# A new order table for an attention, Fourier and feed-forward kernel: TensorE's narrow products stand in fewer, longer runs

## The chip, the core and the metric

The kernel runs on one NeuronCore of a Trainium2 chip. Five engines work side by side, each on its own queue of instructions in a fixed order: TensorE (PE: matrix products; PEld is its loading of weights), VectorE (DVE), ScalarE (ACT), GpSimd (POOL) and SyncE (SP, which here only issues DMAs). They wait for one another through semaphores. The metric is the device time of one execution in microseconds, lower is better.

## The reference

```python
# sliding-window attention, 8 batches, 8 heads, 576 positions, 64 columns
scores = (1.0 / np.sqrt(D)) * np.matmul(q, k.transpose(0, 1, 3, 2))
mask = (rel >= 0) & (rel < 64)
attn = softmax(np.where(mask, scores, -1e9))
x = np.matmul(attn, v)            # as (8, 576, 512)
# Fourier mixing, norm and feed-forward
X = np.fft.fft(np.fft.fft(x, axis=1), axis=2)
u = x + np.real(X)
un = (u - mean(u)) / np.sqrt(var(u) + 1e-6)
out = u + np.maximum(un @ w_ch1, 0.0) @ w_ch2      # 512 -> 2048 -> 512
```

Inputs arrive as float32 (the two weight matrices as float64 bits), the output is float32.

## The kernel before

The 4608 rows of the problem are 36 attention tiles of 128 positions. For each tile and each of two groups g of four heads, `score` (L648 in float32 for tiles 0 to 12, L653 in two float16 parts from tile 13 on) makes the scores psc, DVE adds the mask and takes the maximum (L670), ACT takes the exponential (L678), the result pr is turned around (through TensorE, L689 pp, in the early tiles; as two float16 parts that are made by ACT, DVE or POOL and turned by a DMA in the later ones) into pt, and `av` (L732) multiplies it by the values into pa. After that come `normed` (DVE, L738 to L742), the Fourier transform of each batch (pg L963, pz L997), the norm, and the feed-forward of 18 chunks of 256 rows: a first product ph (L1283; 12 products of 256 columns for one f), the two-part relu hh (ACT L1292, then DVE L1295), and a second product po (L1264; 6 products of 512 columns for one f). Chunk 0 runs it in float32, the others in three float16 passes. In this text the number behind a name is the tile, chunk or batch: psc22_1 is the score of tile 22, group 1.

Two kinds of attention product use only a part of TensorE's array: pa and the later psc work on 128 rows by 64 columns (two products beside each other, for the two halves of a tile), the early psc on 64 by 64. The page writes that as 128*64 and 64*64 behind the name. They are called narrow here, everything else (128*128, and the 97*96 of the Fourier stage) is called full.

What sets the order is written out: `op` records 2900 steps with their reads and writes, `follow` walks them in the order of the table ORDER, and the program is issued in just that order, on all engines. SECOND lists the steps with two possible engines that go to their second one (ACT or DVE, DVE or POOL). `follow` keeps a planned time too; where TensorE is planned to stand idle for more than 0.8 us before the float16 feed-forward begins, the last loop puts products into the gap that serve nothing but TensorE's clock (warm, L1359). Each psum tile comes from a ring of banks: ps (4 banks: scores, pa, turns, Fourier), f1 (2: ph) and f2 (2: po).

Of the kernel before, what the change touches and what calls it, by code (L numbers as in the profile page):

```python
# [58 lines left out]
171 10 0 8 172 1 7 9 4 3 173 174 175 196 176 177 197 180 181 179 178 199 185 182 198 200 201 186 183 222 202 184 187  # L59
11 205 188 191 210 221 189 206 211 226 204 190 203 207 192 247 193 208 224 223 209 212 227 12 13 213 214 16 225 14 230  # L60
2 215 15 246 251 235 216 228 231 236 194 248 17 232 237 217 229 18 21 195 233 218 249 234 250 238 239 272 252 240 255
253 19 241 271 256 20 260 257 26 276 22 277 258 23 219 5 242 220 259 243 261 273 264 274 265 254 262 275 31 27 263 280
24 244 6 281 266 245 282 487 267 268 25 283 278 36 284 285 269 270 28 490 286 488 298 491 299 287 489 289 288 312 290
291 279 303 292 41 492 302 493 293 306 496 512 307 294 497 513 295 316 300 296 304 494 317 308 515 46 498 301 305 313
517 310 538 499 309 322 314 500 37 318 537 505 501 323 319 518 324 51 315 325 502 506 542 47 326 503 514 311 543 540
327 504 32 331 563 33 29 335 56 332 34 320 333 336 321 562 541 337 507 297 516 328 334 508 495 521 329 61 38 42 567
330 52 339 39 338 340 57 519 43 341 509 66 522 343 539 526 523 44 342 35 53 344 71 527 345 30 520 54 524 664 565 48
510 566 49 568 528 76 355 350 529 525 346 546 511 665 347 40 530 351 547 667 58 348 668 352 548 81 62 63 349 549 64
353 550 59 354 532 531 45 369 72 50 77 86 78 370 82 73 564 74 372 371 83 544 84 373 91 533 67 68 375 79 87 69 555 534
551 377 96 556 552 669 689 376 75 88 374 356 553 101 570 554 55 380 60 545 97 690 80 92 98 382 670 93 99 106 535 102  # L70
378 89 357 575 362 381 571 379 65 94 111 70 557 358 694 576 558 692 666 103 95 577 559 385 100 104 359 116 386 695 107
108 572 360 569 383 112 714 109 363 384 121 85 390 117 578 118 536 361 560 113 573 717 119 574 114 105 579 364 126 387
110 580 718 122 123 561 671 673 693 365 715 124 366 581 90 392 367 582 131 115 678 583 391 674 679 127 584 128 393 585
129 120 136 586 125 680 388 130 588 394 132 589 719 389 133 675 395 134 141 590 681 587 396 592 691 591 137 596 400
593 594 138 135 146 598 401 142 139 672 740 143 140 676 597 602 144 677 151 603 720 682 147 145 684 148 698 739 149
595 683 150 397 697 599 368 413 600 414 398 604 415 152 716 153 154 742 402 605 699 156 685 700 416 611 417 686 423
403 612 155 601 613 608 399 424 161 157 405 609 158 606 696 610 425 607 767 687 703 617 688 426 721 743 159 621 404
427 162 166 163 744 160 406 164 618 766 428 165 619 614 429 745 407 430 620 615 768 167 439 168 2020 704 440 169 2016
441 616 622 442 701 170 2017 623 443 705 418 624 2018 444 625 769 2019 419 408 626 770 420 702 627 421 445 2021 772
422 446 723 431 411 706 2026 432 409 433 2027 2022 434 410 455 2023 771 2024 435 456 436 457 875 2032 437 458 628 2025  # L80
438 459 460 447 707 448 461 2030 2028 724 773 449 709 708 725 2031 741 2029 450 878 2033 722 879 728 451 910 726 462
2036 727 452 412 2034 2044 629 876 729 2035 710 2037 453 774 471 454 730 472 463 746 2038 464 473 2042 474 465 466 475
2039 775 476 467 468 477 748 2040 478 469 2043 2041 470 2045 630 479 2048 2046 731 2049 480 636 2047 481 732 2050 631
733 482 734 632 483 2054 735 765 881 484 2056 637 485 2051 633 634 749 2055 2052 2053 750 643 635 2057 753 486 2060
2058 638 754 2059 751 639 711 640 755 2061 756 641 644 642 2062 712 2063 650 759 2066 645 2068 2064 2067 646 2072 736
2069 651 2073 2070 752 2071 652 737 647 747 757 777 2084 2074 648 758 882 649 2076 760 2085 713 657 883 2075 2077 653
911 778 654 2078 761 2082 655 658 656 2079 2083 884 2080 659 2081 762 2086 776 877 2090 738 763 779 2088 660 2087 764
661 781 802 2089 885 782 916 787 662 2094 783 880 788 917 789 2096 784 918 790 2091 785 886 2097 786 2092 791 807 2093
889 792 2095 890 806 2065 891 2102 810 912 811 2098 2100 803 913 945 2099 892 914 895 793 896 795 893 915 2101 794 897
816 796 980 2108 898 797 888 2103 948 780 820 899 919 798 2104 2106 799 804 900 808 2109 949 2105 812 920 2107 805 946  # L90
809 2120 2110 800 950 814 813 930 921 2112 894 817 951 821 931 924 887 2113 818 663 925 822 826 823 2111 926 2121 815
827 983 828 952 829 2122 2123 2124 830 927 831 984 953 903 932 2114 819 1090 835 824 825 985 933 839 836 801 837 981
# [1298 lines left out]
```

## Time and profile before

| what | value |
|---|---|
| runs | 989.87, 994.36, 994.63 us; median 994.36 us |
| profiled execution | 990.8 us, of which the span of the trace is 988.6 us |
| PE busy | 964.2 us, 98% of the span |
| DVE, ACT, POOL busy | 644.1, 367.1, 332.3 us |
| granted TensorE clock, mean over the span | 0.996 |

The page counts an engine as busy from the start of its instructions to their ends. Matmuls are pipelined: the start of one matmul to the start of the next is the time that it costs, while the duration shown for it (0.2 to 0.4 us) overlaps with its neighbours'. So the working of this text goes by starts. [...]

### The profile page before, as it was taken

The page shows a single profiled execution, that of the slowest core. Times are in us where ns is not written, and L with a number is a line of the kernel's source. Part 1 is how long each engine was busy: PE and PEld are TensorE (multiplying, and loading weights), DVE is VectorE, ACT ScalarE, POOL GpSimd, SP SyncE. Part 2 cuts the span into 40 slices and gives each one's busy share as a digit, 9 for nine tenths or more (in the row PEclk, how much of TensorE's full clock was granted, in tenths as well). Part 3 has the DMA queues.
Part 4 walks back from the last instruction along what each step waited for, and adds up shares of the span by engine and source line. Part 5 has one row for each costly group of instructions (what it writes and reads, how often), then busy time and mean ns, then how long its engine had stood idle before and what let it go on. Part 6 is the DMA issues. An engine that isn't in the chain of part 4 may idle for free.

```text
span 988.6 us, 22785 instructions
## 1 busy us (share of the span) xinstructions
PE 964.2 (98%) x8964; PEld 672.2 (68%) x8964; DVE 644.1 (65%) x1827; ACT 367.1 (37%) x853; POOL 332.3 (34%) x675
## 2 busy tenths in 40 slices
PE   7699999999999999999999999999999999999998
PEld 6577667676766676666776667666776677666665
DVE  5699888988768668867658565776756555421111
ACT  5565657844433343334324443224422221111110
POOL 1342152233834541342643264425623331210000
PEclk9899999999999999999999999999999999999999
DMA  9998664526897958778669754876354401320010
GB/s 206 240 236 227 175 175 106 132 59 135 154 195 147 176 86 184 144 170 156 111 145 166 139 125 113 172 141 146 65 132 92 87 1 52 69 43 12 1 43 22
DMA packets 309067, 123.09 MB, mean 125 GB/s; under 512 B 291096, under 2 KB 291224, under 8 KB 308960
## 3 DMA queue, kind: packets, MB, share of 16 engines
q1 hardware_dynamic: 306240, 112.72, 53.9%
q0 software_dynamic: 2720, 8.92, 3.5%
q8 instruction: 70, 1.15, 0.5%
q14 instruction: 37, 0.30, 0.1%
HBM read 54.99 MB, written 14.17 MB: 70 GB/s over the span
## 4 chain that ended last, share of the span: by engine, by line
PE 85%; DMA 6%; DVE 5%; ACT 2%; issue 1%; POOL 1%; SPq 0%; DVEq 0%; POOLq 0%; ACTq 0%
PE ph L1283 36%; PE po L1264 35%; PE pa L732 3%; PE psc L653 2%; PE pz L997 2%; PE pg L963 2%; DMA kn<-in_k 2%; PE psc L648 1%; DMA mt<-md,gix 1%; DMA uhl<-up 1%; DMA qbd<-flex 1%; PE pp L689 1%; PE py L823 1%; PE mt L1040 1%; PE warm L1359 1%
## 5 line engine op out<-in xcount | busy, mean ns | idle before, releaser
L1264 PE MATMUL po<-w1s,hh 128*128 128x512 f16 (+1 forms) x1696 | 426.2, 388 | 1.5 <-ACT hh L1289 0.9
L1283 PE MATMUL ph<-uhl,w0s 128*128 128x256 f16 (+1 forms) x3384 | 424.1, 277 | 1.9 <-DVE hh L1295 1.1
L1283 PEld LDWEIGHTS <-w0s 128*128 128x128 f16 x3264 | 316.5, 98 | 81.2 <-issue 3.5
L1264 PEld LDWEIGHTS <-hh 128*128 128x128 f16 x1632 | 154.5, 98 | 139.6 <-DVE hh L1295 1.0
L1292 ACT ACTIVATE hh<-ph 128x512 f16<-128x512 f32 x136 | 80.9, 595 | 330.1 <-PE ph L1283 252.0
L1295 DVE SCALAR_TENSOR_TENSOR hh<-ph,hh 128x512 f16<-128x512 f32 x136 | 93.4, 687 | 156.7 <-ACT hh L1292 156.5
L678 ACT ACTIVATE pr<-pr,nm 128x128 f32<-128x128 f32 x288 | 91.2, 390 | 43.1 <-DVE nm L670 41.8
L670 DVE CUSTOM_DVE_ANT_0 pr<-psc,mskb 128x128 f32<-128x128 f32 x288 | 65.6, 286 | 23.6 <-PE psc L653 18.9
L1071 POOL DMA_INDIRECT mt<-md,gix x34 | 34.6, 1019 | 112.4 <-DMA md<-mp 49.0
L489 POOL TENSOR_TENSOR flex<-pr,flex 128x128 f16<-128x128 f32 x112 | 49.9, 476 | 54.8 <-ACT flex L479 44.9
L1095 POOL TENSOR_TENSOR rs<-mv,mhalf 128x1 f32<-128x1 f32 x36 | 23.4, 649 | 102.9 <-DVE mv L1091 88.5
L489 POOL TENSOR_TENSOR up<-un,up 128x128 f16<-128x128 f32 x80 | 36.4, 485 | 47.8 <-ACT up L479 36.4
L489 POOL TENSOR_TENSOR flex<-qn,flex 128x128 f16<-128x128 f32 x80 | 36.5, 491 | 28.6 <-ACT flex L479 24.8
L732 PE MATMUL pa<-ve,pt 128*64 128x65 f16 (+1 forms) x760 | 43.6, 207 | 1.9 <-ACT pt L479 0.9
L489 POOL TENSOR_TENSOR flex<-kn,flex 128x128 f16<-128x128 f32 x60 | 27.9, 494 | 48.8 <-ACT flex L479 30.4
L732 PE MATMUL pa<-va,pt 128*64 128x65 f16 (+1 forms) x760 | 43.7, 207 | 0.0
L479 ACT CAST up<-un 128x512 f16<-128x512 f32 x29 | 17.8, 615 | 48.3 <-DVE un L1099 19.3
L489 POOL TENSOR_TENSOR y<-xu 128x128 f32<-128x128 f32 x36 | 19.3, 568 | 44.8 <-DVE xu L742 39.6
L489 POOL TENSOR_TENSOR hs<-h,hs 128x97 f16<-128x97 f32 x56 | 21.4, 415 | 37.5 <-ACT hs L479 32.2
L742 DVE TENSOR_TENSOR xu<-pa,rc 128x256 f32<-128x256 f32 x72 | 30.6, 424 | 2.5
L1318 DVE SCALAR_TENSOR_TENSOR xu<-po,osc,xu 128x512 f32<-128x512 f32 x34 | 24.2, 744 | 11.1 <-PE po L1264 11.1
L653 PEld LDWEIGHTS <-qbd 128*64 128x64 f16 x736 | 21.9, 110 | 13.8 <-issue 13.7
(163 smaller groups left out, 1172.4 us busy)
## 6 DMA issues: line engine op xcount, KB each, us to landing
wd<-in_moe_w_ch SPq DMA_DIRECT2D x20, 512.0 KB, 5.4
out<-xu SPq DMA_DIRECT2D x36, 256.0 KB, 2.6
ve<-va SPq DMA_DIRECT2D x67, 130.0 KB, 3.4
kn<-in_k SPq DMA_DIRECT2D x32, 256.0 KB, 3.6
qn<-in_q SPq DMA_DIRECT2D x32, 256.0 KB, 4.0
flex<-in_moe_w_ch SPq DMA_DIRECT2D x12, 512.0 KB, 7.8
flex<-in_v SPq DMA_DIRECT2D x20, 256.0 KB, 3.3
md<-mp SPq DMA_DIRECT2D x24, 192.0 KB, 2.6
```

Of the source, the lines that this page charges most:

```text
L489: eng.tensor_tensor(out=out[:, k : k + w], in0=in0[:, k : k + w], in1=in1[:, k : k + w], op=al)
L653: nc.tensor.matmul(out, qbd[i][:, jj, h, 64 * z : 64 * z + 64], keys(h, jj), start=(z == 0), stop=(z == 1))
L670: nc.vector.tensor_tensor_reduce(out=t["pr", g][:, hp], in0=t["ps", g][:, hp], in1=mskb[:, m : m + P], scale=-0.125, scalar=3.0e38, op0=AL ...
L678: nc.scalar.activation(pr, pr, AF.Exp, bias=t["nm", g][:, hp : hp + 1], scale=-1.0)
L732: nc.tensor.matmul(pa[sl, hp], pt[:, sl], v_, start=(x == 0), stop=(x == len(mm) - 1))
L742: nc.vector.tensor_tensor(out=xv[:, g::2], in0=pa[:, :, 0:64], in1=rc.to_broadcast([P, 4, 64]), op=ALU.mult)
L1071: nc.gpsimd.indirect_dma_start(out=mts[T], out_offset=None, in_=mds[pb][0 : HR if n < 4 else 2 * HR], in_offset=bass.IndirectOffsetOnAxis( ...
L1264: nc.tensor.matmul(t["po"][i], l_, r_, start=(f == 0 and x == 0), stop=(f == NKF - 1 and x == len(mm) - 1))
L1283: nc.tensor.matmul(ph, l_, r_, start=(x == 0), stop=(x == len(mm) - 1))
L1292: nc.scalar.activation(t["hh", j][:, 0], ph, AF.Relu)
L1295: nc.vector.scalar_tensor_tensor(out=hh[:, 1], in0=ph, scalar=0.0, in1=hh[:, 0], op0=ALU.max, op1=ALU.subtract)
L1318: nc.vector.scalar_tensor_tensor(out=xts[g], in0=t["po"][i], scalar=osc, in1=xts[g], op0=ALU.mult, op1=ALU.add)
```

## The change

ORDER and SECOND hold other numbers; no function changes, and the 2900 steps and what depends on what are the same. All lines behind the tables are one higher in the changed kernel.

```diff
 ORDER = [int(i) for i in """
-171 10 0 8 172 1 7 9 4 3 173 174 175 196 176 177 197 180 181 179 178 199 185 182 198 200 201 186 183 222 202 184 187
+171 8 10 1 9 3 172 7 0 173 174 175 196 176 177 197 180 198 181 199 185 182 178 11 201 186 202 183 200 179 184 187 221
...
 SECOND = {int(i) for i in """
-177 193 200 202 234 238 259 268 293 303 307 312 315 319 321 360 559 595 601 605 607 641 648 655 686 711 713 736 761
+175 188 200 202 250 263 268 275 293 303 307 311 312 315 319 321 360 559 595 601 605 607 641 648 655 686 711 736 761
...
```

Counted in the built programs: narrow products stand in 112 runs before and in 63 now. If 128*128, 128*64 and 64*64 are taken as three kinds, TensorE changes its kind 231 times before and 138 times now; up to the first product of the weights' scale (pw0, L1208, at 143.3 us of the trace) 49 times before and 41 now, behind it 182 and 97. Behind pw0 it goes into a narrow run from a full product 91 times before and 47 now, out of one as often, and from one narrow kind to the other never before and 3 times now. Of the warm products there are 80 before and 93 now, 14 of them ahead of the first other product in both. Of the steps with two engines, 234 ran on DVE and 263 do now: 21 come from POOL and 8 from ACT on balance; up to about 240 us they are 41 before and 39 now. SP issues the same number of DMAs.

Each piece below stands in the order of its engine; a line of "..." leaves rows out, mostly further products and weight loads of the same step.

TensorE, where the scores of tile 22 and the values of tile 20 lie, before:

```order
L1264 MATMUL po6_1_6224<-w1s_85,hh6_0_6134 128x512
...
L653 MATMUL psc22_1_6238<-kst_79,qbd0_76 64x128
...
L1264 MATMUL po6_0_6223<-w1s_85,hh6_0_6134 128x512
...
L732 MATMUL pa20_1_6275<-ve0_82,pt20_1_6183 64x65
...
L732 MATMUL pa20_0_6308<-ve0_82,pt20_0_5810 64x65
...
L1283 MATMUL ph6_5_6333<-uhl6_4734,w0s_84 128x256
...
L653 MATMUL psc22_0_6356<-kst_79,qbd0_76 64x128
...
L1264 MATMUL po6_0_6223<-w1s_85,hh6_1_6231 128x512
```

and now:

```order
L1265 MATMUL po6_1_6197<-w1s_85,hh6_0_6120 128x512
...
L654 MATMUL psc22_0_6253<-kst_79,qbd0_76 64x128
...
L733 MATMUL pa20_1_6273<-ve0_82,pt20_1_6149 64x65
...
L654 MATMUL psc22_1_6306<-kst_79,qbd0_76 64x128
...
L733 MATMUL pa20_0_6324<-ve0_82,pt20_0_5855 64x65
...
L1265 MATMUL po6_0_6196<-w1s_85,hh6_1_6204 128x512
```

Four narrow steps in three runs have become one run of four; the products po6 and ph6_5 that stood between them stand ahead of it or behind it.

DVE, between the second parts of hh6_1 and hh6_2 of the same stretch (psc22 are the masks, rc20 the sums of tile 20), before:

```order
L1295 SCALAR_TENSOR_TENSOR hh6_1_6231<-ph6_1_6154,hh6_1_6231 128x512
L670 ISA pr22_1_6237,nm22_1_6268<-psc22_1_6238,mskb_71 128x128
...
L738 TENSOR_SCALAR rc20_0_6346<-pa20_0_6308 128x4
...
L742 TENSOR_TENSOR xu20_6307<-pa20_0_6308,rc20_0_6346 128x4x64
...
L742 TENSOR_TENSOR xu20_6307<-pa20_1_6275,rc20_1_6351 128x4x64
L1295 SCALAR_TENSOR_TENSOR hh6_2_6300<-ph6_2_6121,hh6_2_6300 128x512
```

and now:

```order
L1296 SCALAR_TENSOR_TENSOR hh6_1_6204<-ph6_1_6127,hh6_1_6204 128x512
L490 TENSOR_TENSOR flex_78<-qn23_5887,flex_78 128x8x128
...
L1089 BN_STATS st17_6237<-xu17_4882 128x6
...
L484 CAST flex_78<-pr21_1_5901 128x4x128
L490 TENSOR_TENSOR flex_78<-pr21_1_5901,flex_78 128x4x128
L671 ISA pr22_0_6252,nm22_0_6300<-psc22_0_6253,mskb_71 128x128
...
L1100 TENSOR_SCALAR un17_6349<-xu17_4882,mv17_6239,rs17_6298 128x512
L1296 SCALAR_TENSOR_TENSOR hh6_2_6271<-ph6_2_6154,hh6_2_6271 128x512
```

The sums of tile 20 moved behind hh6_2, and splits of tiles 21 and 23 and the norm of tile 17 moved in ahead of it.

TensorE in chunk 13, from the last first product of its fifth pair (ph13_4) to the second product that needs the relu of that pair (hh13_4), before:

```order
L1283 MATMUL ph13_4_11765<-uhl13_9905,w0s_84 128x256
...
L823 MATMUL py35_11806<-ident_69,y35_11788 128x128 x4
...
L1264 MATMUL po13_0_11551<-w1s_85,hh13_3_11709 128x512
...
L1283 MATMUL ph13_5_11711<-uhl13_9905,w0s_84 128x256
...
L1264 MATMUL po13_0_11551<-w1s_85,hh13_3_11709 128x512
...
L1283 MATMUL ph13_6_11845<-uhl13_9905,w0s_84 128x256
...
L1264 MATMUL po13_0_11551<-w1s_85,hh13_4_11818 128x512
```

and now:

```order
L1284 MATMUL ph13_4_11666<-uhl13_9871,w0s_84 128x256
...
L1265 MATMUL po13_0_11485<-w1s_85,hh13_3_11598 128x512
...
L824 MATMUL py35_11794<-ident_69,y35_11780 128x128 x4
...
L1265 MATMUL po13_0_11485<-w1s_85,hh13_4_11791 128x512
```

Between the two stood two steps of po13, one of ph13_5, one of ph13_6 and the turn py35; now one step of po13 and py35 are left.

## Rows read from the trace of the kernel before

**Rows 1.** The page, part 1: busy us (share of the span) and instructions by engine.

```profile
PE 964.2 (98%) x8964; PEld 672.2 (68%) x8964; DVE 644.1 (65%) x1827; ACT 367.1 (37%) x853; POOL 332.3 (34%) x675
```

**Rows 2.** Busy time by stretch: length, PE, PEld, DVE, ACT, POOL, PEclk, DMA, GB/s.

```profile
0.00:50.00 50.00, 37.23 (x492) 28.97 (x496) 31.59 (x142) 26.98 (x69) 10.45 (x34) 0.93 0.96 221
50.00:100.00 50.00, 47.51 (x468) 35.54 (x461) 48.30 (x147) 28.67 (x80) 19.63 (x35) 1.00 0.88 236
...
240.00:500.00 260.00, 259.46 (x2668) 180.12 (x2666) 190.90 (x548) 101.78 (x230) 118.81 (x250) 1.00 0.79 154
```

**Rows 3.** TensorE's waits from 143 us to 988 us: total us, times, longest us.

```profile
PE ph L1283 <- DVE hh L1295: 1.1, 2, 0.8
PE ph L1283 <- DMA uhl<-up: 0.7, 1, 0.7
PE po L1264 <- DVE hh L1295: 0.5, 1, 0.5
```

**Rows 4.** TensorE's timeline in pure feed-forward: start us, length us, what, count.

```profile
403.23 1.47 PE L1283 MATMUL ph<-uhl,w0s 128*128 128x256 f16 x12
404.54 1.46 PE L1264 MATMUL po<-w1s,hh 128*128 128x512 f16 x6
405.83 1.47 PE L1283 MATMUL ph<-uhl,w0s 128*128 128x256 f16 x12
```

**Rows 5.** TensorE's timeline, a run of three narrow steps.

```profile
511.12 1.46 PE L1264 MATMUL po<-w1s,hh 128*128 128x512 f16 x6
512.51 0.64 PE L653 MATMUL psc<-kst,qbd 128*64 128x128 f16 x16
512.98 0.19 PE L732 MATMUL pa<-ve,pt 128*64 128x65 f16 x1
...
513.33 0.20 PE L732 MATMUL pa<-va,pt 128*64 128x65 f16 x1
513.36 0.62 PE L653 MATMUL psc<-kst,qbd 128*64 128x128 f16 x16
```

**Rows 6.** TensorE's timeline, single narrow steps between full ones.

```profile
429.51 0.19 PE L732 MATMUL pa<-va,pt 128*64 128x65 f16 x1
429.63 1.48 PE L1283 MATMUL ph<-uhl,w0s 128*128 128x256 f16 x12
431.05 0.64 PE L653 MATMUL psc<-kst,qbd 128*64 128x128 f16 x16
431.62 1.47 PE L1264 MATMUL po<-w1s,hh 128*128 128x512 f16 x6
```

**Rows 7.** TensorE's timeline in an early tile: from 128*64 to 64*64.

```profile
140.23 0.22 PE L732 MATMUL pa<-ve,pt 128*64 128x65 f32 x1
...
140.29 0.22 PE L732 MATMUL pa<-va,pt 128*64 128x65 f32 x1
140.44 1.10 PE L648 MATMUL psc<-kst,qbd 64*64 64x128 f32 x32
```

**Rows 8.** Groups of instructions, TensorE, 0 to 82 us: the warm products.

```profile
L1359 PE MATMUL warm<-ident 128*128 128x256 f16 x80 | 13.8, 306 | 2.1 <-POOL ident masks.py:199 2.1
```

**Rows 9.** Busy time by stretch around the half-clock stretch, columns as in rows 2.

```profile
37.00:42.60 5.60, 3.02 (x31) 1.85 (x29) 5.39 (x27) 3.98 (x11) 0.00 (x0) 1.00 0.98 275
42.60:49.40 6.80, 5.77 (x48) 4.68 (x48) 3.90 (x11) 2.53 (x7) 2.67 (x8) 0.50 0.87 224
```

**Rows 10.** DVE's splits and casts of attention parts: duration ns min/median/max.

```profile
L489 DVE TENSOR_TENSOR flex<-pr,flex x18: 679/690/916, 240.6 to 775.1; 128x512 f16<-128x512 f32 x18
L483 DVE CAST flex<-pr x16: 414/427/655, 240.1 to 774.4; 128x512 f16<-128x512 f32 x16
```

**Rows 11.** Timeline of TensorE, ACT and DVE at the end: the last relu.

```profile
979.01 3.19 PE L1264 MATMUL po<-w1s,hh 128*128 128x512 f16 x14
979.21 0.60 ACT L1292 ACTIVATE hh<-ph 128x512 f16<-128x512 f32 x1 [4.61 <-PE ph L1283]
979.84 0.69 DVE L1295 SCALAR_TENSOR_TENSOR hh<-ph,hh 128x512 f16<-128x512 f32 x1 [4.52 <-ACT hh L1292]
```

247 rows, old and new, of tables (ORDER, SECOND) are left out of this document.

## The prediction

> **What bounds the kernel now.** I read the share of busy time first, then the same by stretch, then TensorE's waits, then its timeline. PE is busy for 964.2 us of the span of 988.6 us [rows 1]. By stretch this splits in two: in the first 50 us it is busy for 37.2 us, while from 240 to 500 us it is busy for 259.5 of 260 us [rows 2]. From 143 us to the end TensorE waits only four times, 2.3 us in total [rows 3]. So behind some 140 us the time is the sum of what TensorE's products cost one after the other; ahead of that it is a chain of attention steps through DVE, ACT and DMA, in which TensorE stands idle now and then.
>
> Busy does not mean that the products follow at their best pace, so I go by starts. In pure feed-forward 12 first products take 404.54 - 403.23 = 1.31 us and 6 second products 405.83 - 404.54 = 1.29 us [rows 4]. Where a narrow run comes next the same 6 take 512.51 - 511.12 = 1.39 us [rows 5] and the same 12 take 431.05 - 429.63 = 1.42 us [rows 6]: going in costs 0.09 to 0.11 us. Inside the run, 16 scores followed by values take 512.98 - 512.51 = 0.47 us, and the step back from values to scores shows no gap: 513.36 - 513.33 = 0.03 us, the same as between two pairs of values [rows 5]. The same 16 scores followed by a full product take 431.62 - 431.05 = 0.57 us, and after values the full product starts 429.63 - 429.51 = 0.12 us after the last of them instead of 0.03 [rows 6]: going out costs 0.09 to 0.10 us. No wait is shown at any of these; it is paid at every one, and by the busy rows it looks like work. The page's idle time can't show what this change removes.
>
> The third kind behaves the same: from values (128*64) to early scores (64*64) it is 140.44 - 140.29 = 0.15 us, where values follow one another in 140.29 - 140.23 = 0.06 us [rows 7], so a change between two narrow kinds costs 0.09 us as well. [...] Counting narrow against full alone there would be 98 changes fewer (224 to 126) and 98 x 0.095 = 9.3 us to gain at most; counting kinds, as the rows do, there are 93 and 8.8 us.
>
> **The change part by part.** *Changes of kind behind 143 us.* Entries from a full product fall from 91 to 47, exits as well, and 3 changes between narrow kinds are new. 44 x 0.09 + 44 x 0.10 - 3 x 0.09 = 3.96 + 4.40 - 0.27 = 8.1 us less. TensorE is the bound there and nothing else waits at these points, so all of it is on the path. With the upper readings (0.11 and 0.10) it is 9.0 us, with the lower (0.09 and 0.09) 7.7 us.
>
> *Changes of kind ahead of 143 us.* They fall from 49 to 41: 8 x 0.095 = 0.8 us. TensorE has 12.8 us of idle time in the first 50 us [rows 2] that can swallow this; I count half, 0.4 us less.
>
> *Warm products.* 13 more, at 13.8 us / 80 = 0.17 us each [rows 8], are 2.2 us. Where TensorE waits at that place they fill the wait and cost nothing; where its input is there already they delay the chain in full. The trace can't tell which; between 0 and 2.2 us I take 1.1 us more. What they are for shows at 37 us: TensorE was busy for 3.0 of 5.6 us, and then the granted clock was 0.50, the lower of its two levels, for 6.8 us, with 5.8 us of work in it [rows 9]. Without that stretch up to 5.77 / 2 = 2.9 us go; another one like it costs 2.9 us. I count neither, and keep both ends.
>
> *New waits behind 143 us.* Longer runs take DVE and ACT more work at once. Three checks on the order. First the psum banks: the longest float16 run has four steps, and ps has four banks, so no run needs more than there are. Second the way from scores to values, which goes through DVE, ACT, POOL and a turning DMA on SP's queue: adding up TensorE's steps at the paces above, the shortest in float16 is 11.3 us before (tile 13, which did not wait) and 12.2 us now. SP's issues are in another order, but the room that they are given is kept. Third the relu: the end of the trace shows hh ready at 979.84 + 0.69 = 980.53 us, 1.52 us after the product behind ph has started at 979.01 [rows 11]. Added up the same way, the shortest distance from the end of a first product to the second product that needs its relu is 2.59 us before, at ten of 136 places 2.6 us, and none of these waits. Now four are shorter: 1.73 us (the piece of chunk 13 shown with the change: one step of po13, 1.29 us, and the four turns of py35), 1.96, 2.35 and 2.36 us. They still exceed 1.52 us, but one split of 0.69 us ahead on DVE [rows 10] makes the first two late, by 0.48 and 0.25 us (1.52 + 0.69 = 2.21); the other two only with more than that ahead. Against 2.3 us of waits that may go or stay, I take 0.5 us more; the bounds are 2.3 us less and 3.2 us more (0.8 us, the longest of today's waits of this kind [rows 3], at all four).
>
> *Work that moves to DVE.* 21 steps come from POOL and 8 from ACT, at 0.69 and 0.43 us [rows 10]: 14.5 + 3.4 = 17.9 us of DVE. Up to 240 us the count falls by two, where DVE is at its fullest, 48.3 of 50 us [rows 2]; behind it DVE has 190.9 of 260 us in use and takes it. What hides it is that room, so nothing on the path; what it costs without that cover is a rival below.
>
> *Sum.* Against the profiled execution, 990.8 us: - 8.1 - 0.4 + 1.1 + 0.5 = - 6.9, so 983.9 us. The three runs before are 989.87, 994.36 and 994.63 us; the profiled one belongs with the lowest, the median lies 3.6 us above. Since the new median may fall with either, I put a third of that on top: **985 us**, 0.9% under the median.
>
> **The rivals.** *Given back in waits.* The runs are merged at the price of a tighter early chain and later relus: all 13 warm products exposed (2.2), one more half-clock stretch (2.9), all four tight places late (3.2). That is - 8.1 + 8.3 = + 0.2, with the same allowance 992 us, no change. For it: 13 more warm products mean that the planner sees more idle time early. Against it: the shortest way from scores to values has not shrunk, and three of the mishaps must meet.
>
> *DVE becomes the bound: the slower end.* DVE works its queue in order, and the relu's second part stands in it. In the stretch shown with the change, between hh6_1 and hh6_2, DVE had masks and two sums before and now has three splits or casts, a norm and masks. If the 17.9 us moved there each delay a relu that TensorE stands before, the time is 985 + 17.9 = 1003 us. It decides slower only from 14.3 us of the 17.9 on (994.36 x 1.005 = 999.3), that is if four of five moved steps hit. Against it: DVE's room behind 240 us, and 2.59 us or more at 132 of 136 places.
>
> *The cost stays.* If the 0.1 us did not belong to the change of kind but to a first product of a step, it would be paid just as often: 993 us, no change. Against it: the step from values to scores in one run shows none.
>
> *The early chain gets shorter too.* The half-clock stretch goes (2.9), all warm products fill waits (1.1 less than I count), the rest of the early saving shows (0.4): 980.6 us. For it: the warm products now stand at 22 places instead of 19. [...]
>
> **How the numbers follow.** Forecast 0.63; given back 0.16; early chain shorter 0.12; DVE 0.05; cost stays 0.04. About 0.5% (5 us) is what a measurement of this kernel can tell from no change: faster is below 989.4 us, slower above 999.3. Faster: 0.58 of the forecast's 0.63 (a single early mishap of 4.5 us takes it over the line), 0.12, and 0.04 of the second: 0.74. Slower: 0.05, and 0.01 for mishaps that add up: 0.06. The same: 0.20. Range: 8.1 us of gain with the bounds of the early part (4.4 less than I count as in the last rival, 4.4 more with another half-clock stretch, exposed warm products and nothing of the early saving) and of the late waits (2.8 less, 2.7 more) reaches from 977.8 to 992.1: **978 to 992 us**. The lower and upper reading of the changes of kind (0.4 less gain, 0.9 more) lie inside that. Above it lie the DVE rival, half of the two rivals of no change and a little of the forecast, below it little.
>
> **What would show it.** Right: TensorE's timeline in the late part with 0.47 us for scores and no gap inside runs of four, busy time of PE less by some 8 us from 143 us on, the same number of products apart from 13 warm ones. Waits of PE behind 143 us stay under 5 us. Wrong: po and ph rows that wait for DVE's hh more than ten times (the DVE rival); a second stretch of PEclk 0.50, or more than 3 us of added idle time in the first 100 us (given back); 0.57 us for scores inside a run (the cost stays).

## The result

The changed kernel takes 982.65 us (median of 6 runs, 979.58 to 986.12) where the kernel before takes 993.43 us (6 runs, 989.87 to 994.63). The ratio is 0.9899 with a 95% interval of 0.9866 to 0.9931: 1.0% faster. The profiled execution took 983.69 us with a span of 981.9 us, against 990.8 and 988.6 us before. The forecast of 985 us, its range, and the 983.9 us that the sum gave for a profiled execution held. Two of the terms behind them did not: they were off by 1.5 and 1.4 us in opposite directions. A third, the early part, fits in this execution alone.

The page of the changed kernel, part 1 (busy us, share, instructions), to be set against [rows 1]:

```profile
PE 953.9 (97%) x8977; PEld 674.8 (69%) x8977; DVE 659.0 (67%) x1859; ACT 362.8 (37%) x845; POOL 303.4 (31%) x597
```

TensorE runs 13 products more and is busy for 10.3 us less. DVE is busy for 14.9 us more and POOL for 28.9 us less. The same by stretch, columns as in [rows 2], where PEclk is the granted TensorE clock as a share of the full one (its records in the traces of before and after hold 1.00 and 0.50 alone); the last line is everything behind 143 us:

```profile
0.00:50.00 50.00, 35.40 (x475) 29.08 (x476) 30.52 (x136) 24.58 (x64) 15.31 (x39) 0.93 0.93 206
50.00:100.00 50.00, 45.11 (x482) 35.01 (x479) 47.12 (x143) 29.29 (x81) 21.78 (x37) 1.00 0.85 231
240.00:500.00 260.00, 258.21 (x2678) 181.66 (x2676) 195.85 (x562) 102.23 (x233) 106.68 (x218) 1.00 0.80 153
143.00:981.90 838.90, 831.05 (x7733) 582.63 (x7732) 543.28 (x1480) 282.58 (x630) 255.73 (x504) 1.00 0.55 111
```

and the last line's counterpart of the kernel before:

```profile
143.00:988.60 845.60, 838.96 (x7729) 580.46 (x7727) 526.93 (x1438) 285.21 (x634) 290.02 (x592) 1.00 0.54 110
```

Behind 143 us the stretch is 845.6 - 838.9 = 6.7 us shorter and TensorE's busy time falls by 7.9 us, so the saving is in what looks like work. DVE gains 16.4 us of work there. TensorE's waits behind 143 us in the changed kernel (total us, times, longest us):

```profile
PE po L1265 <- DVE hh L1296: 2.2, 2, 1.6
PE ph L1284 <- DVE hh L1296: 1.2, 3, 0.7
PE ph L1284 <- DMA uhl<-up: 0.3, 1, 0.3
```

They are 3.7 us in six places, against 2.3 us in four [rows 3]. Inside a run no gap shows between two narrow steps. TensorE's timeline of the run of four that the order shows (scores and values of tiles 22 and 20):

```profile
427.67 1.46 PE L1265 MATMUL po<-w1s,hh 128*128 128x512 f16 x6
429.06 0.64 PE L654 MATMUL psc<-kst,qbd 128*64 128x128 f16 x16
429.53 0.19 PE L733 MATMUL pa<-ve,pt 128*64 128x65 f16 x1
...
429.88 0.20 PE L733 MATMUL pa<-va,pt 128*64 128x65 f16 x1
429.91 0.62 PE L654 MATMUL psc<-kst,qbd 128*64 128x128 f16 x16
430.36 0.19 PE L733 MATMUL pa<-ve,pt 128*64 128x65 f16 x1
...
430.71 0.19 PE L733 MATMUL pa<-va,pt 128*64 128x65 f16 x1
430.83 1.04 PE L1265 MATMUL po<-w1s,hh 128*128 128x512 f16 x4
```

The scores take 429.53 - 429.06 = 0.47 us at the head of the run and 430.36 - 429.91 = 0.45 us inside it, a difference that comes back in the account of the prediction. The step from values back to scores is 0.03 us, the pace of two pairs of values. The run pays once going in (429.06 - 427.67 = 1.39 us instead of 1.29) and once going out (430.83 - 430.71 = 0.12 us instead of 0.03). Before, these four steps lay in three runs.

The start of the program went the other way, which I had not seen. TensorE in the kernel before:

```profile
2.08 3.14 PE L1359 MATMUL warm<-ident 128*128 128x256 f16 x14 [2.08 <-POOL ident masks.py:199]
5.04 0.61 PE L546 MATMUL pk<-ident,kn 128*128 128x128 f32 x4
```

and in the changed one:

```profile
2.91 3.17 PE L1360 MATMUL warm<-ident 128*128 128x256 f16 x14 [2.91 <-POOL ident masks.py:199]
5.87 1.06 PE L547 MATMUL pk<-ident,kn 128*128 128x128 f32 x4
```

TensorE starts 0.83 us later, because POOL now fills other constants before the identity that the first products need. The four products pk also take 1.06 us instead of 0.61: the trace's record of the granted clock at 1.00 begins at 8.35 us, where before it began at 5.05 us (in the kernel before, four products pk at 43.40 us, inside its stretch at 0.50, took 1.09 us). POOL's timeline in the changed kernel:

```profile
1.66 0.53 POOL L453 MEMSET ve<- 64x520 f32 x1
2.24 0.12 POOL L450 MEMSET va<- 128x8 f32 x1
2.28 0.21 POOL masks.py:197 MEMSET ident<- 128x128 f32 x1
2.56 0.29 POOL masks.py:199 TENSOR_SCALAR_AFFINE_SELECT ident<-ident 128x128 f32<-128x128 f32 x1
```

### The profile page after: what moved, and what is told of

The parts are those of the page before. It is cut to its first block, busy times and chain, and to the rows that moved or that the text cites. A ratio compares the mean times of both kernels' runs of the same rounds, so it can differ in the third digit from the quotient of the medians.

```text
span 981.9 us, 22750 instructions
## 1 busy us (share of the span) xinstructions
PE 953.9 (97%) x8977; PEld 674.8 (69%) x8977; DVE 659.0 (67%) x1859; ACT 362.8 (37%) x845; POOL 303.4 (31%) x597
## 4 chain that ended last, share of the span: by engine, by line
PE 84%; DVE 6%; DMA 4%; issue 3%; POOL 2%; ACT 1%; SPq 1%; DVEq 0%; POOLq 0%; ACTq 0%
PE ph L1284 36%; PE po L1265 36%; PE pa L733 2%; PE pz L998 2%; PE pg L964 2%; PE psc L654 2%; DMA kn<-in_k 2%; DMA mt<-md,gix 1%; PE pp L690 1%; DMA flex<-in_v 1%; PE pk L547 1%; DVE pr L671 1%; DVE un L1100 0%; PE py L824 0%; PE warm L1360 0%
## 5 line engine op out<-in xcount | busy, mean ns | idle before, releaser
L1265 PEld LDWEIGHTS <-hh 128*128 128x128 f16 x1632 | 156.7, 98 | 140.5 <-DVE hh L1296 3.1
L671 DVE CUSTOM_DVE_ANT_0 pr<-psc,mskb 128x128 f32<-128x128 f32 x288 | 65.2, 285 | 23.4 <-PE psc L654 19.4
L490 POOL TENSOR_TENSOR flex<-qn,flex 128x128 f16<-128x128 f32 x96 | 45.7, 510 | 43.5 <-ACT flex L480 28.2
L490 POOL TENSOR_TENSOR flex<-pr,flex 128x128 f16<-128x128 f32 x76 | 37.4, 522 | 55.0 <-ACT flex L480 21.5
L733 PE MATMUL pa<-ve,pt 128*64 128x65 f16 (+1 forms) x760 | 40.4, 206 | 1.6 <-ACT pt L480 0.8
L733 PE MATMUL pa<-va,pt 128*64 128x65 f16 (+1 forms) x760 | 40.5, 206 | 0.0
L490 POOL TENSOR_TENSOR up<-un,up 128x128 f16<-128x128 f32 x56 | 24.3, 462 | 49.6 <-ACT up L480 37.6
L998 PE MATMUL pz<-g,ds__75 97*96 97x257 f16 (+3 forms) x240 | 30.1, 273 | 1.7 <-DVE nm L671 1.1
L1319 DVE SCALAR_TENSOR_TENSOR xu<-po,osc,xu 128x512 f32<-128x512 f32 x34 | 24.3, 744 | 9.1 <-PE po L1265 9.1
L490 POOL TENSOR_TENSOR fs<-f,fs 128x97 f16<-128x97 f32 x44 | 20.7, 500 | 29.9 <-ACT fs L480 27.5
L998 PEld LDWEIGHTS <-ds__75 97*96 97x96 f16 (+1 forms) x240 | 26.7, 123 | 4.1 <-DVE nm L671 1.4
```

The lines of the kernel that those rows point to most:

```text
L490: eng.tensor_tensor(out=out[:, k : k + w], in0=in0[:, k : k + w], in1=in1[:, k : k + w], op=al)
L671: nc.vector.tensor_tensor_reduce(out=t["pr", g][:, hp], in0=t["ps", g][:, hp], in1=mskb[:, m : m + P], scale=-0.125, scalar=3.0e38, op0=AL ...
L733: nc.tensor.matmul(pa[sl, hp], pt[:, sl], v_, start=(x == 0), stop=(x == len(mm) - 1))
L998: nc.tensor.matmul(pz[:M, c0:c1], ds_[:NJ, a, c[0] : c[0] + c[1]], t["g", gi][:, b_, c0:c1], start=(x == 0), stop=(x == len(mm) - 1),)
L1265: nc.tensor.matmul(t["po"][i], l_, r_, start=(f == 0 and x == 0), stop=(f == NKF - 1 and x == len(mm) - 1))
```

## How the traces are taken apart

All comparisons of traces below go by the starts of TensorE's products. *Early* is from its first product other than a warm one to pw0; *late* is from pw0 to the start of its last step (the first of that step's products). *Waits* are the places behind pw0 where the way from one step's start to the next exceeds the usual pace (with its change of kind) by more than 0.12 us; these include places for which the page shows no releaser, so they sum to more than the rows of waits. *Rest* is late without waits. All in us, one profiled execution each; the kernels are explained with the experiments.

| kernel | first product | pw0 | early | changes of kind, late | late | waits (places) | rest |
|---|---|---|---|---|---|---|---|
| before | 5.04 | 143.31 | 138.28 | 182 | 839.59 | 2.96 (4) | 836.63 |
| before_again | 5.04 | 143.81 | 138.77 | 182 | 838.89 | 2.27 (4) | 836.62 |
| early_a | 5.88 | 143.10 | 137.22 | 182 | 836.93 | 0.29 (1) | 836.64 |
| split | 5.87 | 142.38 | 136.51 | 163 | 839.85 | 5.50 (8) | 834.34 |
| merge | 5.04 | 143.93 | 138.89 | 124 | 837.13 | 6.99 (9) | 830.14 |
| after | 5.87 | 144.34 | 138.47 | 97 | 831.90 | 4.89 (8) | 827.01 |
| early_b | 5.04 | 144.20 | 139.17 | 97 | 830.13 | 3.19 (3) | 826.94 |
| nowarm | 5.87 | 143.95 | 138.07 | 97 | 829.12 | 2.15 (4) | 826.96 |
| ident_first | 4.31 | 141.01 | 136.70 | 97 | 833.75 | 6.78 (8) | 826.97 |
| ident_nowarm | 4.31 | 144.26 | 139.96 | 97 | 828.98 | 1.88 (3) | 827.10 |
| second_b | 5.87 | 143.48 | 137.61 | 97 | 836.00 | 8.99 (11) | 827.01 |

The last column is the result in one view. Traces with the same late order, and so the same number of changes of kind, agree in it to 0.2 us, whatever the early order, the engines chosen or the waits. Between before and after it is (836.63 - 827.01) / 85 = 0.113 us for each change.

The early column does not hold still like that. The three narrow kernels below have the early part of the changed kernel too; their pw0 lies at 143.16, 142.50 and 143.14 us. So in six traces with the new early part and the same engines in it (after, split, early_a and these three) pw0 lies between 142.38 and 144.34 us, median 143.12, and the changed kernel's own is the latest; in four with the old one (before, before_again, merge, early_b) it lies between 143.31 and 144.20 us, median 143.87.

## Experiments

**split: the runs broken up again.** Theory: the number of changes of kind sets the time. Rival: something else in the new table (other engines, other buffer times) brings the gain. In the changed kernel's table 34 late places inside narrow runs get a step of full products between them, moved there from nearby; all else stays. The changes behind pw0 rise from 97 to 163.

```diff
-702 422 2026 411 431 2022 432 412 723 2023 433 709 409 771 455 2027 434 456 628 435 2024 716 436 457 458 437 707 697
+702 422 2026 411 431 2022 432 412 723 2023 433 2027 709 409 771 455 434 456 628 435 2024 716 436 457 458 437 707 697
...
```

> The changed kernel with 34 of its late narrow runs broken up again: a full step that stood behind two narrow ones now stands between them, nothing else is moved, SECOND stays. Behind the first product of the weights' scale TensorE changes its kind 163 times instead of 97. Theory (each change costs 0.095 us on the path): that part takes 831.9 + 66 x 0.095 = 838.2 us in the profile, the time is some 6 us above the changed kernel, about 989 us. Rival (the gain came from what else the search moved, the changes of kind are only where it shows): the part stays within 2 us of 831.9, the time at 981 to 985 us.

Measured: 989.6 us (median of 12 runs, 986.97 to 996.71), ratio to the kernel before 0.9975 (0.9957 to 0.9993); 7 us of the gain are gone. The rest column goes from 827.01 to 834.34 us, 7.3 us for 66 changes, 0.111 us each. Its timeline at one of the broken runs:

```profile
432.18 0.62 PE L654 MATMUL psc<-kst,qbd 128*64 128x128 f16 x16
432.73 1.47 PE L1265 MATMUL po<-w1s,hh 128*128 128x512 f16 x6
434.12 0.22 PE L733 MATMUL pa<-ve,pt 128*64 128x65 f16 x1
```

The scores are 0.55 us again instead of 0.45 to 0.47, and the full step is 434.12 - 432.73 = 1.39 us instead of 1.29: one change out, one in. The theory stands.

**merge: the change made by hand in the old table.** 29 local moves in the table of the kernel before put narrow steps next to each other; the early part and the choice of engines stay. 182 changes become 124.

```diff
-438 459 460 447 707 448 461 2030 2028 724 773 449 709 708 725 2031 741 2029 450 878 2033 722 879 728 451 910 726 462
+438 459 460 447 707 448 461 709 2030 2028 724 773 449 708 725 2031 741 2029 450 878 2033 722 879 728 451 910 726 462
...
```

> The kernel before with SECOND as it was, and 29 local moves on TensorE alone that put a narrow step next to another one, past one or two full steps: behind the first product of the weights' scale 124 changes of kind instead of 182. Theory: that part falls from 839.6 by 58 x 0.095 = 5.5 us to 834.1 us, plus up to 2 us of new waits since nothing else was fitted to the moves; time 988 to 990 us against 993.4. Rival (merging pays only with a new plan for the other engines): waits for hh and for scores eat it, the part stays at 838 us or more.

Measured: 986.98 us (6 runs, 984.48 to 988.95), ratio 0.9943 (0.9926 to 0.9961), 1 us below what was expected. The rest column falls by 6.5 us for 58 changes, 0.112 us each, but the waits grow from 3.0 to 7.0 us and take more than half of it back in this execution. Waits of TensorE behind 143 us in merge:

```profile
PE po L1264 <- DVE hh L1295: 1.9, 1, 1.9
PE pa L732 <- DVE nm L670: 1.2, 1, 1.2
PE ph L1283 <- DVE hh L1295: 1.1, 1, 1.1
PE ph L1283 <- DMA uhl<-up: 0.8, 1, 0.8
PE pa L732 <- DMA pt<-flex: 0.2, 1, 0.2
```

Two rows wait for hh and one for the way from scores to values (nm): the two costs that the prediction weighed for longer runs. The rival of a gain given back in waits is real for moves that do not look at who waits.

**early_b and early_a: the two halves swapped.** early_b has the old table up to pw0 and the new one behind it, early_a the reverse, each with the engines that belong to its halves.

> The order of before up to the first product of the weights' scale, with its choice of engines, and the order of the changed kernel behind it. Theory: the late part is as in the changed kernel, 831.9 us within 1 us; the early part is as before, about 138.3 us from TensorE's first product, and since the two early parts differ by 0.2 us the time is that of the changed kernel within 2 us, 981 to 985 us. Rival (the early order carries a part of the gain): 3 us or more slower than the changed kernel. Rival (the early order of the changed kernel with 13 more warm products costs): 2 us or more faster.

Measured: 983.21 us (6 runs, 981.77 to 988.52), ratio 0.9921 (0.9899 to 0.9943). The late part alone makes all of the gain that can be told apart.

> The other way round: the order and engines of the changed kernel up to the first product of the weights' scale, those of before behind it. Theory: late part 839.6 us within 1 us, the time that of the kernel before within 2 us (991 to 995 us). Rival (the early order carries a part of the gain): 990 us or less. Rival (it costs): 996 us or more.

Measured: 988.48 us (7 runs, 986.33 to 989.49), ratio 0.9957 (0.9938 to 0.9977). This missed what was expected: the new early part ahead of the old late part is faster by 0.4%, some 4 us, where the late part keeps all its changes of kind. Its trace says where: the rest is the old 836.64 us; pw0 comes 0.2 us earlier than before, and the old late order, with waits of 3.0 and 2.3 us in the two traces of before, has 0.29 us here. That is 0.2 + 2.7 = 2.9 us in the profiled execution. Why the waits behind pw0 depend on what ran ahead of it is shown for one of them: ahead of the wait at 294.90 us in before (0.54 us) DVE had stood for 1.95 us in front of the addition xu, until its load mt landed; in before_again it stood there for 1.24 us and in early_a not at all, and neither trace waits at that place. For the others it stays open. It also means that "late" is not independent of "early", so the medians of the two halves don't add up to that of the whole.

**narrow1, narrow2_next, narrow2_apart: the price of a change by itself.** The last four chunks have no attention products beside them. They have 64 second steps of six products. In each of these steps one product (narrow1), two neighbours (narrow2_next) or two that are apart (narrow2_apart) are done as two products over 64 columns of weights each, into the two halves of the same output. The arithmetic is the same. Theory: only changes of kind cost. Rival: narrow products cost by themselves, so that two cost twice as much wherever they stand.

```diff
+NARROW = {(1, 1), (1, 2)}
...
-                        nc.tensor.matmul(
-                            t["po"][i], l_, r_, start=(f == 0 and x == 0), stop=(f == NKF - 1 and x == len(mm) - 1)
-                        )
+                        halves = 2 if c >= 14 and (i, x) in NARROW else 1
+                        for jj in range(halves):
+                            w = P // halves
+                            nc.tensor.matmul(
+                                t["po"][i][w * jj : w * jj + w], l_[:, w * jj : w * jj + w], r_,
+                                start=(f == 0 and x == 0), stop=(f == NKF - 1 and x == len(mm) - 1),
+                            )
```

This is narrow2_next; narrow1 has {(1, 2)} and narrow2_apart {(0, 2), (1, 2)} as NARROW.

> The changed kernel, where in chunks 14 to 17 the last of the six products of each second step (64 steps) is issued as two narrow ones beside each other, one for each half of the output rows; the sums are the same. Theory (a change of kind costs 0.09 to 0.10 us): two changes for each step, 64 x 0.19 = 12.2 us more in those chunks, and a full pace (0.22 us) for the pair. Rival (the cost belongs to the narrow product or to the first product of a step, not to the change): 64 x 0.1 = 6 us or nothing.

> As the kernel with one narrow product in each second step of chunks 14 to 17, but with the last two of the six narrow, next to each other. Theory: still two changes for each step, so the same 12.2 us within 1 us. Rival (a narrow product costs by itself): twice the cost of one narrow product.

> As the kernel with two narrow products in each second step of chunks 14 to 17, but with the third and the sixth of the six narrow, so that full ones stand between. Theory: four changes for each step, 64 x 0.38 = 24.3 us. Rival (a narrow product costs by itself): the same as with the two next to each other.

Measured, one run each: 993.01, 992.46 and 1010.03 us. From the first product of chunk 14 to the start of the last second step the changed kernel takes 178.39 us, narrow1 192.70, narrow2_next 192.70 and narrow2_apart 207.03 us. That stretch holds 63 of the 64 changed steps. One narrow product in each of them is two changes, 14.31 / 126 = 0.114 us each. Two neighbours, twice as many narrow products, cost the same to 0.01 us. Two apart are 28.64 / 252 = 0.114 us. The stretches grew by more than the 12.2 and 24.3 us expected, as the price of a change had been taken too low. The step of po reads so, in narrow2_next:

```profile
902.35 1.58 PE L1269 MATMUL po<-w1s,hh 128*128 128x512 f16 x8
903.86 0.50 PE L1289 MATMUL ph<-uhl,w0s 128*128 128x256 f16 x3
```

and in narrow2_apart:

```profile
902.16 1.81 PE L1269 MATMUL po<-w1s,hh 128*128 128x512 f16 x8
903.90 0.50 PE L1289 MATMUL ph<-uhl,w0s 128*128 128x256 f16 x3
```

Both have eight products in the step (a narrow pair counts as two), with the arithmetic of six full ones; one takes 903.86 - 902.35 = 1.51 us and the other 1.74 us, where the plain step takes 1.29 us [rows 4]. Neither shows a wait: the cost lies in lengths. The rival falls, and with it the rival of the prediction by which the cost belonged to the first product of a step: the number of steps is the same in all four kernels.

**nowarm: the warm products behind the first 14 left out.** They compute nothing that is used. If they delay the chain, the early part gets shorter; if they fill waits, nothing changes, or the clock falls more often.

```diff
-            if early and o.eng == "PE" and gap > WARM[0]:
+            if early and o.eng == "PE" and gap > WARM[0] and o.idx == 174:
```

> The changed kernel without its 79 warm products behind the first 14. If the warm products are exposed, 79 x 0.17 = 13 us of TensorE goes and the time falls by several us. If they only fill waits, the early part keeps its length; then what is left is the clock: without them TensorE is busy less in the first 85 us and the granted clock should show more than one stretch at 0.50 there, each worth up to 3 us, so 983 to 992 us. Forecast of the theory: no faster than 981 us.

Measured: 980.37 us (6 runs, 978.42 to 984.2), ratio 0.9881 (0.9862 to 0.9899), against 0.9899 (0.9866 to 0.9931) for the changed kernel: not to be told apart. Of what was expected neither the several microseconds faster nor the 983 to 992 us came. In the profiled execution early is 0.4 us shorter, with one half-clock stretch more (columns as in [rows 2]; the first line is the stretch ahead of it):

```profile
65.90:71.50 5.60, 3.53 (x62) 2.98 (x63) 5.50 (x24) 2.17 (x5) 5.13 (x9) 1.00 0.84 225
71.50:74.90 3.40, 3.40 (x12) 2.40 (x11) 3.33 (x12) 3.09 (x12) 0.00 (x0) 0.51 1.04 304
```

So far from all of the 79 products' 13 us lie on the path. The 0.4 us itself is less than the 2 us by which traces with the same early part differ, so whether they are worth anything on balance stays open.

**ident_first: the late start mended.** The identity (step 0 of the table) moves from the ninth place to the second, so that POOL makes it ahead of the other constants.

```diff
-171 8 10 1 9 3 172 7 0 173 174 175 196 176 177 197 180 198 181 199 185 182 178 11 201 186 202 183 200 179 184 187 221
+171 0 8 10 1 9 3 172 7 173 174 175 196 176 177 197 180 198 181 199 185 182 178 11 201 186 202 183 200 179 184 187 221
```

> The changed kernel with one step moved: the identity matrix is made on POOL ahead of the small fills instead of behind them. In the changed kernel TensorE's first warm product waits for it until 2.9 us (before: 2.1 us), the first turn pk stands at 5.87 us (before: 5.04), and the granted clock goes up 3.3 us later. Theory: pk stands at 5 us or earlier, the clock goes up by 5 to 6 us again, and 1 to 2 us of the early part come back: 980.5 to 982 us against 982.65. Rival (the start is hidden by the loads and the attention chain behind it): the first products move, the first product of the weights' scale stays at 143 to 144.3 us, the time at 982 to 984 us.

Measured: 978.99 us (5 runs, 976.17 to 982.23), ratio 0.9859 (0.984 to 0.9878); the expectation had 980.5 to 982 us. TensorE starts with

```profile
1.35 3.17 PE L1360 MATMUL warm<-ident 128*128 128x256 f16 x14 [1.35 <-POOL ident masks.py:199]
4.31 0.94 PE L547 MATMUL pk<-ident,kn 128*128 128x128 f32 x4
```

5.87 - 4.31 = 1.56 us earlier than in the changed kernel, and pw0 comes 3.3 us earlier, at 141.01 us, which is 1.4 us ahead of the earliest of the six traces with the changed kernel's early part. The half-clock stretch is shorter as well, 3.4 us where the changed kernel has 6.8 us (the line ahead of each is the stretch before it), in ident_first:

```profile
36.90:42.50 5.60, 1.52 (x13) 1.00 (x11) 5.53 (x20) 3.39 (x10) 0.00 (x0) 1.00 1.04 281
42.50:45.90 3.40, 3.40 (x34) 3.07 (x33) 0.36 (x2) 1.99 (x5) 2.72 (x8) 0.50 1.04 252
```

and in the changed kernel:

```profile
36.90:42.50 5.60, 3.45 (x59) 2.61 (x54) 5.40 (x29) 2.69 (x9) 1.01 (x3) 1.00 1.12 250
42.50:49.30 6.80, 4.53 (x44) 4.22 (x44) 3.04 (x7) 3.06 (x9) 2.73 (x8) 0.50 0.92 222
```

This version is faster than the kernel before by 1.4%. That it beats the changed kernel too is likely, 3.7 us by the medians, but the two intervals touch (0.9866 to 0.9878), so the size is open, and so is how much of the 1.56 us at the start reaches the end.

**ident_nowarm: both edits.**

> The changed kernel with the identity made first and without the 79 warm products behind the first 14. If the two add up: 1 to 2 us below the kernel without warm products (980.4), 978.5 to 979.5 us. If neither is on the path: 980 to 983 us. Behind the first product of the weights' scale 827.2 us plus 1 to 5 us of waits.

Measured: 978.53 us (4 runs, 977.09 to 980.68), ratio 0.9854 (0.9836 to 0.9872), the same as ident_first. The profiled execution has three half-clock stretches (from 23.4, 40.4 and 71.1 us, 3.4, 6.8 and 3.4 us long) and an early part of 139.96 us, 3.3 us more than ident_first; the waits behind pw0 are 4.9 us less. In this execution what was won at the start was gone by pw0.

**second_b: the order new, the choice of engines old.** The table SECOND of the kernel before under the changed kernel's ORDER.

> The order table of the changed kernel with the choice of engines (SECOND) of the kernel before: 234 steps of two engines on DVE instead of 263. Theory (the moved work lies in DVE's room, but the order was fitted to it): no change of kind differs, so the late part is 827.2 us plus waits, and waits grow by no more than 3 us: 982 to 986 us. Rival (the engine choice carries a good part of the gain): the late part has 5 us or more of further waits, 988 us or more. Rival (DVE's further 18 us cost): 980 us or less.

Measured: 984.18 us (6 runs, 982.1 to 986.93), ratio 0.9911 (0.9894 to 0.9928). The rest is 827.01 us as in the changed kernel, the waits are 8.99 us in 11 places instead of 4.89 in 8, and among them stand waits for POOL that the changed kernel doesn't have:

```profile
PE py L823 <- POOL y L489: 1.8, 1, 1.8
PE pg L963 <- POOL hs L489: 0.6, 1, 0.6
```

So the steps that went from POOL to DVE are no loss; by the profile they spare waits, but the medians differ by 1.5 us, less than the intervals can tell apart.

**before_again: a second profile of the kernel before**, to see what two executions of one kernel share.

> The kernel before once more, for a second profile of it. If the waits behind the first product of the weights' scale belong to the order, they come again at the same places (214, 294, 646, 753 us) with 4 us in total and that part takes 839.6 us; if they differ from execution to execution, the part lies between 836 and 840 us with waits elsewhere. The changes of kind cost the same in both.

Measured: 990.61 us with a span of 988.4 us; the rest is 836.62 us against 836.63. Of the four waits of the first trace three come again at the same places; the one of 0.54 us at 294.90 us does not, and a short one of 0.3 us near 864 us is new. The half-clock stretch is 3.4 us long instead of 6.8.

## Why the prediction was right, and where it was not

**The bound.** Right. Behind some 140 us the time is the sum of TensorE's products, and the page's idle time does not show what the change removes: with 6.7 us less span TensorE's busy time is 7.9 us less and its waits are more.

**Changes of kind behind 143 us: mis-sized, -9.6 us instead of -8.1.** The term took 0.09 us in and 0.10 us out as single rows had shown. By the rest column it is 9.62 us for 85 changes, 0.113 us each, outside the upper reading of 9.0 us too. The rows allowed 0.10 and 0.11 us for going in (1.39 against 1.29 us [rows 4, 5], 1.42 against 1.31 us [rows 4, 6]), and I took 0.09, the lowest reading. Even the upper readings, 0.11 in and 0.10 out, make 0.21 us for a run, where the column gives 0.226. What these miss lies inside the run: I took 0.47 us as the price of 16 scores, but that is the price at the head of a run. Scores behind another narrow step take 0.45 us, as the run of four above shows, so the first narrow step of a run is 0.02 us dearer (over the whole late part of the changed kernel 0.471 us in the median of 20 against 0.449 us in 6, where a narrow step follows; values 0.274 against 0.253 us). A run thus costs about 0.09 us in the full step ahead of it, 0.02 in its first step, 0.10 at its end and 0.01 in the full step behind it. The 3 new changes between narrow kinds can't be told apart in the column; counting them as changes fits it to 0.1 us.

The runs agree in where the price falls: 0.11 us a change, the same for two narrow products between two changes as for one. What takes the time at a change no trace here shows.

**The early part.** The sum had +0.7 us (-0.4 and +1.1), and in the two profiled executions pw0 came 144.34 - 143.31 = 1.03 us later. That this fits is luck. The start is 0.83 us later for the late identity, which I overlooked because I compared what stands on TensorE and DVE and not POOL's first ten instructions, though the diff's first line shows step 0 in another place. And over all traces pw0 comes earlier with the new early part and not later, 143.12 against 143.87 us in the median, though the two ranges overlap: from TensorE's first product on it is some 1.6 us shorter (137.24 against 138.83 us). So +0.7 has the wrong sign as far as these ten traces tell. The 13 added warm products can't be singled out: without 79 of them early is 0.4 us shorter in one trace, with 3.4 us more at half clock, which can hide 3.4 / 2 = 1.7 us; if each of the 79 costs the same that makes (0.4 + 1.7) x 13 / 79 = 0.35 us, as an estimate, well under the spread. The half-clock stretch of [rows 9] stayed in the changed kernel's own trace, 6.8 us long from 42.5 us on, as the sum had it; with the same early part it was 3.4 us in three of the other traces (split and the two narrow2), 3.4 us twice in narrow1, and 3.4 and 6.8 us in early_a.

**Late waits: mis-sized, +1.9 us instead of +0.5 in this execution.** They stayed under 5 us, as said. Of the four places at which the prediction found hh tight, one was late, in chunk 5 (1.96 us by adding up). ACT, DVE and TensorE there in the changed kernel (other rows left out):

```profile
398.11 0.60 ACT L1293 ACTIVATE hh<-ph 128x512 f16<-128x512 f32 x1 [2.91 <-PE ph L1284]
398.87 0.69 DVE L1087 TENSOR_TENSOR xu<-xu,mt 128x512 f32<-128x512 f32 x1 [2.73 <-DMA mt<-md,gix]
399.59 0.69 DVE L1089 BATCH_NORM_STATS2 st<-xu 128x6 f32<-128x512 f32 x1
399.81 0.60 PE L1265 MATMUL po<-w1s,hh 128*128 128x512 f16 x2
400.32 0.18 DVE L1091 BATCH_NORM_AGGREGATE mv<-st 128x2 f32<-128x6 f32 x1
400.54 0.15 DVE L1092 TENSOR_SCALAR mv<-mv 128x1 f32<-128x1 f32 x1
400.61 0.76 DVE L490 TENSOR_TENSOR yT<-py 128x512 f32<-128x512 f16 x2
401.28 0.68 DVE L1296 SCALAR_TENSOR_TENSOR hh<-ph,hh 128x512 f16<-128x512 f32 x1
402.02 1.04 PE L1265 MATMUL po<-w1s,hh 128*128 128x512 f16 x4 [1.61 <-DVE hh L1296]
```

The mechanism is the one described, with another length: not one split of 0.69 us stands ahead of hh, but an addition, the statistics of a norm and a step on a turned tile (yT), from 398.87 to 401.28 us, while ACT's part of the relu was done at 398.71; the wait is 1.6 us where 0.25 was reckoned. The first row of DVE shows what set it: DVE had stood idle for 2.73 us until the load mt landed, with all of this queued behind. In nowarm the same load is there earlier against TensorE's steps, and the relu goes through without delay:

```profile
395.72 0.69 DVE L1087 TENSOR_TENSOR xu<-xu,mt 128x512 f32<-128x512 f32 x1 [1.26 <-DMA mt<-md,gix]
398.74 0.69 DVE L1296 SCALAR_TENSOR_TENSOR hh<-ph,hh 128x512 f16<-128x512 f32 x1 [0.53 <-ACT hh L1293]
399.81 1.47 PE L1265 MATMUL po<-w1s,hh 128*128 128x512 f16 x6
```

Over the six traces with the new late order it goes in step: the addition starts 1.2, 1.6 and 2.1 us ahead of the last product before the wait in after, ident_first and second_b, which wait 1.6, 1.2 and 0.7 us, and 4.0 to 4.6 us ahead of the same product in the other three, which don't wait. The tightest place, in chunk 13 (1.73 us), and the two in chunks 6 and 7 did not wait at all. Other waits of the changed kernel lie where adding up showed 2.6 us or more (540.80 us, 0.54 us). So distance alone ranks the places badly; what DVE holds at that moment decides, and with it when a load lands that DVE's queue waits for. Over the six traces with the new late order the waits come to 1.9 to 9.0 us, so +1.9 is the figure of one execution: the five traces with the changed kernel's late engines average 3.8 us, the two of before 2.6, which makes +1.2.

**Sum.** -9.6 + 1.9 = -7.7 us behind pw0 (the sum had -7.6) and +1.0 ahead of it (+0.7): -6.7 against -6.9 us. The number is right because two errors of 1.5 us cancelled and because this execution's early part was the longest of its kind.

**The step to the median.** The allowance of a third of 3.6 us was not needed: the profiled execution of the changed kernel lies 1.0 us above its median, that of before 2.6 us below its own. The medians differ by 10.8 us, the profiled executions by 7.1; the interval (6.9 to 13.3 us) holds both. With the averages over the traces the sum would be -9.6 + 1.2 - 0.7 = -9.1 us, an estimate that lies nearer to the medians than the pair of profiled executions does.

**The rivals.** DVE as the bound fell: it has 16.4 us more work behind 143 us (17.9 were reckoned) and works 195.85 of 260 us from 240 to 500 us. The rival of the first product of a step fell by narrow2_next. Given back in waits happened for a small part here, and for over half of the gain in the profile of merge. The early chain did not get shorter in the changed kernel's own trace; over the ten traces it did by some 0.7 us at pw0, far from the rival's 4.4 us.

**Still open.** Why most of the old late order's waits are gone in early_a, and why its median gains some 4 us where early_b's lies within 0.6 us of the changed kernel's; what the earlier start in ident_first is worth at the end; what the warm products are worth.

## What to carry to other kernels

Where TensorE is the bound, count how often it goes between narrow and full products and put narrow steps side by side: here a change took 0.11 us and did not show as idle time. Look for such costs with starts of neighbouring products, and size them with a kernel that adds a known number of them, as a few rows came out 15% low here: they had missed that the first narrow step of a run is dearer than the next. When an order is made anew, look at the first ten instructions of every queue, and at what stands ahead of the one short instruction that the bound engine waits for, a step that waits for a load above all, not at the distance alone.

## What was new about the hardware

A change between a full and a narrow product costs 0.111 to 0.114 us in four ways of measuring (before and after, split, merge, narrow products in feed-forward), the same with two neighbouring narrow products as with one. In none of these does it show as a wait.

Two executions of the same order differ in the early part: the half-clock stretch near 43 us was 6.8 us long in one trace of the kernel before and 3.4 us in the other, and with the new early part pw0 came at 142.4 to 144.3 us in six traces. Over the six traces with the new late order the waits behind pw0 went from 1.9 to 9.0 us (with the old choice of engines the most, but 6.8 us without that too) while the rest stayed within 0.2 us. One profiled execution therefore gives the rest to 0.2 us, the early part to about 2 us, and the waits to some microseconds.
